# A list scheduler that also orders the opening pair of token blocks, with table loads and a transfer limit in its model

## The chip, the cores and the metric

The kernel runs on one core of one Trainium2 chip. The metric is device time in microseconds (us): the median of the runs of one kernel. Each run takes one launch; nothing is computed on the host but layouts.

## What is computed

B = 4 batches, N = 6080 tokens, C = 256 channels. The reference, cut to what matters:

```python
qn = q / (norm(q, axis=1) + 1e-6)          # over the 6080 tokens
kn = k / (norm(k, axis=1) + 1e-6)
s  = kn.transpose(0, 2, 1) @ qn / tau      # 256 x 256 for each batch
a  = exp(s - s.max(-1));  a /= a.sum(-1) + 1e-9
x  = (v @ a).reshape(24320, 256)
h  = x @ w_in                              # w_in 256 x 2048, float64
g  = 0.5 * h * (1 + erf(h / sqrt(2)))
out = g @ w_out                            # w_out 2048 x 256, float64
```

## The kernel before, in words

**Numbers in two parts.** Each float32 operand is split into a high and a low part of a narrower type (fp32r), and a product is three matmuls: lo x hi, hi x hi and hi x lo. The two weight matrices arrive as float64, and are narrowed on the device into such pairs by *narrow steps* on DVE and ACT (L522 to L539: clamp, square, integer masks and shifts, cast, subtract, add; the results are `wi`, `win` or `wo`). A narrow step's temporary is `nt` at first and later, by turns, `kqc` and `osb`.

**Folding the attention away.** Batch b's softmax matrix (256 x 256) is multiplied into w_in (`w_group(b, g)`: products L717 to L719 into PSUM, scaling L722, split into `wh`/`wl` at L709/L710, further sums and splits L748 to L761). So a token block needs only v times this product, gelu, and the product with w_out.

**The order of the work.** First come the raw loads, norms and scores of batch 0 (loads L395, products L421, copies of `po` L440) and its softmax, up to about 63 us. Then:

1. `w_group(0, 0)`, then *pair 0*: the first two blocks of 512 tokens of batch 0, computed by plain products. It is done in 8 units u, one for each 256 of the 2048 hidden columns: `plain_products(u)` (L836 to L838, operands `vhi` and `wh`/`wl`), gelu into a high part (L845) and in full (L846) on ACT, the low part `los` on DVE (L847), and one unit later `pair_out(u)` (L970 to L972, with the output weights `wo`). Between the units stand narrow steps for the weights still wanted (`narrow_unit`, `load_unit` for the raw loads at L505) and `w_group(0, 1..3)`. The finished weights are also written to HBM: `keep_in` and `keep_out` (L1096).
2. The *plan*: all other token blocks, chunk by chunk and column group by column group, with a fast seven-product form of matrix multiplication (`chunk_ops` L892 to L894; sums on DVE; gelus L919 and L922; `chunk_out` L1009 to L1011 and L1025 to L1027). The first chunk of the plan is (0, 2). While it runs, DVE makes forms of the output weights (L587) that are kept in `keep_out` and later read by `load_part` (L571) through a ring of four `wo` buffers, 503 loads of 512 KB. `win` is loaded by `load_win` (L551), v by `load_v` (L781). Scores and softmax of batches 1 to 3 are spread over it; softmax needs ACT's Exp (L669) and Sqrt, the blocks need Gelu, and these live in different activation tables.

**What sets the order.** Up to the plan, the order on each engine comes from the order of emission, from `tc.high_priority()` and from `behind(mark)`, which lets a group be issued only after a marked instruction. The plan's instructions are then reordered by class `Order`: `learn` assigns names to ring slots, `arrange` collects dependences (ring slots among them) and costs from `cost`, with PE kept in program order; `latest` derives deadlines backwards from PE's nominal times; `run` does list scheduling over PE, ACT, DVE and SP, in which a transfer takes its bytes by BANDWIDTH and DMA_LAT ns of latency, and transfers run one behind the other; `schedule` repeats it 24 times with deadlines moved ahead where PE stalled, and takes the best. The result is fixed as dependences of each instruction on the one ahead of it on its engine. Instructions of the plan come behind everything emitted earlier on their engine.

Of the kernel before, what the change touches and what calls it, by code (L numbers as in the profile page):

```python
# [78 lines left out]
class Order:  # L79
# [32 lines left out]
    def cost(self, ins, reads, writes):  # L112
        n = max([x[3] for x in reads + writes] + [1])
        psum = any(x[0][0] in ("pa", "pb", "px", "pz", "po0", "po1", "po2", "po3") for x in reads)
        if ins.engine == PE:
            k = reads[0][3] if reads else 1
            if ins.ins[0].dtype == F32:
                return (max(1.69 * k, 112.0),) * 2
            return .4167 * k + 3 + 1.5 * (k <= H), .4167 * k + 170
        if ins.engine == DVE:  # L120
            t = n / .96 + 66
            if type(ins).__name__ == "InstTensorCopy" and not psum:
                t = n / 1.92 + 66
            return t, t + 90
# [58 lines left out]
    def schedule(self, todo, preds, costs):  # L183
# [4 lines left out]
        self.preds, self.costs = preds, costs  # L188
        self.succs = [[] for _ in range(n)]
# [56 lines left out]
    def run(self, late):  # L246
# [5 lines left out]
        for a in range(n):  # L252
            if not left[a]:
                known[self.engine[a]].append(a)
        free, order, slip, dma, events = [0.0] * 4, [], 0.0, 0.0, [0.0]
        while len(order) < n:
# [3 lines left out]
            for e in range(4):  # L260
                if free[e] > now or not known[e]:
                    continue
# [15 lines left out]
                free[e] = now + self.costs[pick][0]  # L278
# [5 lines left out]
                for b, d in self.edges[pick]:  # L284
                    t = dma + DMA_LAT / 2 if d is None else now + d
# [13 lines left out]
BANDWIDTH, DMA_LAT, DMA_LATE = 320.0, 2000, 6000  # L299
# [26 lines left out]
def channel_attention_gelu_ffn(ctx, tc, qk, kqt, vt, tau, w_in, w_out, out):  # L326
# [222 lines left out]
    def load_win(b, g):  # L549
        new_win(b, g)  # L550
        nc.sync.dma_start(out=f32(wins[b, g]), in_=keep_in[g])  # L551
# [226 lines left out]
    def load_v(b, p):  # L778
        t0, n = PAIRS[p]
        raw = pv.tile([P, NCT, 2 * NT], F32, name="v_raw")  # L780
        nc.sync.dma_start(out=raw[:, :, :2 * n],  # L781
                          in_=vt[:, b * N + t0:b * N + t0 + 2 * n].rearrange("(t p) n -> p t n", p=P))
        vraw[b, p] = raw
# [391 lines left out]
    with tc.high_priority(), behind("fill"):  # L1175
        w_group(0, 0)
# [5 lines left out]
    def extras(w):  # L1182

        if w in (0, 2, 4):
            with behind("product"):
                w_group(0, w // 2 + 1)
# [14 lines left out]
    for u in range(NU):  # L1201
# [4 lines left out]
        for _ in range(paces[u] if u < len(paces) else 0):  # L1206
            with behind(*(["gelu"] if u == 0 else [])):
                narrow_unit()
# [224 lines left out]
    body = nc.cur_bb.bb.instructions  # L1433
    start = len(body)
# [4 lines left out]
    todo, preds, costs = order.arrange(list(body), start)  # L1439
    latest = {e: [i.name for i in list(body)[:start] if i.engine == e] for e in (PE, ACT, DVE, SP)}  # L1440
# [43 lines left out]
```

## Time and profile before

| | |
|---|---|
| median of 3 runs (lowest, highest) | 2091.68 us (2085.11, 2091.8) |
| the profiled execution, its own time | 2087.38 us |
| its span | 2085.4 us (2.0 lie around it) |
| mean granted TensorE clock | 0.995 |
| instructions | 40663 |
| PE, DVE, ACT busy | 2039.9, 1857.6, 1621.0 us |
| moved by DMA | 475.30 MB, mean 228 GB/s |

PE is TensorE's matmul, PEld its weight load, DVE VectorE, ACT ScalarE, SP the engine that issues all transfers (`SPq` its queue). A row of the timeline gives start, duration, engine, line, operation, output <- input with shape, and in brackets the idle time ahead of it with what ended it. In a table of waits, "PE po L970 <- DVE wo L539: 4.4, 1, 4.4" says that PE's products for `po` at L970 waited for DVE's `wo` made at L539 for 4.4 us in total, once, at most 4.4. PEclk is the granted TensorE clock, 1.00 being full speed. Line numbers in rows of before are those of the kernel before; in the changed kernel the same lines stand 8 to 12 further down.

### The profile page before, as it was taken

To read this page: it belongs to the slowest core of one execution; us is meant where nothing else is said; L and a number is where in the kernel's file an instruction comes from. 1 tells how busy PE (TensorE), PEld (TensorE's weight loads), DVE (VectorE), ACT (ScalarE), POOL (GpSimd) and SP (SyncE) were. 2 spreads that over 40 slices of the span, in tenths; PEclk is the share of its full clock that TensorE was granted. 3 is DMA by queue.
4 is the path that set the end of the run, shared out by engine and by line. 5 is a ranking of instruction groups with operands and counts; after the bars stand their busy time and mean duration, and the time that the engine had idled before them with its cause. 6 is when DMAs were issued, how large, how long until landed. Compare 5 with 4: busy or idle time off the path is not lost.

```text
span 2085.4 us, 40663 instructions
## 1 busy us (share of the span) xinstructions
PE 2039.9 (98%) x15958; PEld 1967.0 (94%) x15958; DVE 1857.6 (89%) x2733; ACT 1621.0 (78%) x2718; POOL 1.3 (0%) x8
## 2 busy tenths in 40 slices
PE   9889999999999999999999999999999999999999
PEld 7778899999999999999999999999999999999999
DVE  6997899998899999999889899999988998898897
ACT  6665788888888888887888777777787777777775
POOL 0000000000000000000000000000000000000000
PEclk9999999999999999999999999999999999999999
DMA  9547777777777678777687666666556556566655
GB/s 377 183 126 249 238 272 242 270 260 251 251 270 267 223 250 272 238 265 245 211 278 263 206 217 215 219 209 212 199 175 219 183 195 209 196 197 211 198 191 165
DMA packets 151695, 475.30 MB, mean 228 GB/s; under 512 B 15440, under 2 KB 25680, under 8 KB 149456
## 3 DMA queue, kind: packets, MB, share of 16 engines
q1 hardware_dynamic: 151504, 472.71, 67.0%
q8 instruction: 125, 2.05, 0.4%
q14 instruction: 66, 0.54, 0.1%
HBM read 435.16 MB, written 37.49 MB: 227 GB/s over the span
## 4 chain that ended last, share of the span: by engine, by line
PE 83%; DVE 7%; ACT 4%; DMA 4%; issue 2%; SPq 0%; DVEq 0%; ACTq 0%
PE po L1027 9%; PE po L1026 9%; PE po L1025 9%; PE pb L892 4%; PE pb L894 4%; PE pb L893 4%; PE pa L892 4%; PE pa L894 4%; PE pa L893 4%; PE po L1009 3%; PE po L1011 3%; PE po L1010 3%; PE pz L894 2%; PE pz L893 2%; PE pz L892 2%; DMA v_raw<-vt 2%
## 5 line engine op out<-in xcount | busy, mean ns | idle before, releaser
L1027 PE MATMUL po<-los,wo 128*128 128x256 f32 (+1 forms) x1890 | 520.9, 276 | 1.0 <-DVE los L943 0.8
L1025 PE MATMUL po<-his,wo 128*128 128x256 f32 (+1 forms) x1890 | 520.5, 275 | 0.8 <-issue 0.8
L1026 PE MATMUL po<-his,wo 128*128 128x256 f32 (+1 forms) x1890 | 520.0, 275 | 0.0
L925 DVE TENSOR_TENSOR los<-gs,his 128x512 fp32r<-128x512 f32 (+1 forms) x601 | 406.7, 683 | 83.0 <-ACT gs L919 71.0
L1025 PEld LDWEIGHTS po<-his,wo 128*128 128x128 f32 x1890 | 362.9, 192 | 2.8 <-ACT e L669 0.9
L1027 PEld LDWEIGHTS po<-los,wo 128*128 128x128 f32 x1890 | 363.1, 192 | 2.0 <-DVE los L943 1.5
L1026 PEld LDWEIGHTS po<-his,wo 128*128 128x128 f32 x1890 | 363.1, 192 | 0.5
L943 DVE TENSOR_TENSOR los<-gs,his 128x1024 fp32r<-128x1024 f32 (+1 forms) x270 | 326.7, 1211 | 16.3 <-ACT his L939 14.0
L939 ACT CAST his<-gs 128x1024 fp32r<-128x1024 f32 (+1 forms) x270 | 281.3, 1043 | 64.6 <-DVE gs L936 59.5
L892 PE MATMUL pa<-vhi,wl 128*128 128x256 f32 (+1 forms) x920 | 254.2, 276 | 8.1 <-ACT gs L919 7.3
L892 PE MATMUL pb<-vhi,wl 128*128 128x256 f32 (+1 forms) x920 | 254.6, 277 | 4.8 <-DVE pz L906 1.4
L893 PE MATMUL pb<-vhi,wh 128*128 128x256 f32 (+1 forms) x920 | 253.4, 275 | 0.0
L894 PE MATMUL pa<-vlo,wh 128*128 128x256 f32 (+1 forms) x920 | 253.3, 275 | 0.0
L893 PE MATMUL pa<-vhi,wh 128*128 128x256 f32 (+1 forms) x920 | 253.3, 275 | 0.0
L894 PE MATMUL pb<-vlo,wh 128*128 128x256 f32 (+1 forms) x920 | 253.3, 275 | 0.0
L932 DVE TENSOR_TENSOR gs<-gs 128x1024 f32<-128x1024 f32 (+1 forms) x135 | 163.8, 1214 | 31.6 <-ACT gs L919 27.5
L892 PEld LDWEIGHTS pa<-vhi,wl 128*128 128x128 f32 x920 | 176.5, 192 | 13.4 <-ACT gs L919 8.3
L922 ACT ACTIVATE his<-px 128x512 fp32r<-128x512 f32 (+1 forms) x184 | 109.0, 592 | 101.7 <-PE px L894 98.6
L892 PEld LDWEIGHTS pb<-vhi,wl 128*128 128x128 f32 x920 | 176.7, 192 | 10.0 <-DVE pz L906 2.6
L893 PEld LDWEIGHTS pa<-vhi,wh 128*128 128x128 f32 x920 | 176.6, 192 | 3.7
L893 PEld LDWEIGHTS pb<-vhi,wh 128*128 128x128 f32 x920 | 176.7, 192 | 2.5
L894 PEld LDWEIGHTS pb<-vlo,wh 128*128 128x128 f32 x920 | 177.0, 192 | 0.0
(284 smaller groups left out, 5147.3 us busy)
## 6 DMA issues: line engine op xcount, KB each, us to landing
wo<-keep_out SPq DMA_DIRECT2D x503, 512.0 KB, 4.4
raw<-qk SPq DMA_DIRECT2D x95, 512.0 KB, 6.4
kqc<-kqt SPq DMA_DIRECT2D x72, 512.0 KB, 5.1
wo<-keep_out SPq DMA_DIRECT2D x135, 256.0 KB, 3.9
v_raw<-vt SPq DMA_DIRECT2D x20, 1024.0 KB, 7.7
out<-osb SPq DMA_DIRECT2D x40, 512.0 KB, 5.1
win<-keep_in SPq DMA_DIRECT2D x12, 1024.0 KB, 7.4
keep_in<-win SPq DMA_DIRECT2D x4, 1024.0 KB, 4.5
```

What stands on the lines that cost most here:

```text
L892: nc.tensor.matmul(o, wls[g][:, a, q], paired(vh[:, at, :h]), start=start, stop=False, skip_group_check=True)
L893: nc.tensor.matmul(o, whs[g][:, a, q], paired(vh[:, at, :h]), start=False, stop=False, skip_group_check=True)
L894: nc.tensor.matmul(o, whs[g][:, a, q], paired(vl[:, at, :h]), start=False, stop=stop, skip_group_check=True)
L922: nc.scalar.activation(out=slot(name)[0], in_=t[SOURCE[name]], func=AF.Gelu)
L925: tt(out=slot(name)[1], in0=whole(name), in1=f32(slot(name)[0]), op=ALU.subtract)
L932: tt(out=g4[:, 0:2], in0=g4[:, 1:3], in1=g4[:, 0:2], op=ALU.subtract)
L939: nc.scalar.copy(out=views[1][:, 2 - 2 * i:4 - 2 * i], in_=views[0][:, 2 * i:2 * i + 2])
L943: tt(out=views[2][:, at], in0=views[0][:, 2 * i:2 * i + 2], in1=f32(views[1][:, at]), op=ALU.subtract)
L1009: nc.tensor.matmul(o, w[:, 1, q], mh, start=start, stop=False, skip_group_check=True)
L1025: nc.tensor.matmul(o, w[:, 1, q], mh, start=starts and q == 0, stop=False, skip_group_check=True)
L1026: nc.tensor.matmul(o, w[:, 0, q], mh, start=False, stop=False, skip_group_check=True)
L1027: nc.tensor.matmul(o, w[:, 0, q], ml, start=False, stop=stops and q == 1, skip_group_check=True)
```

## The change

Five things, in 142 lines of diff:

1. The scheduled part begins at `w_group(0, 0)` (`opened`) instead of at the plan. `high_priority` and `behind` are dropped from `w_group(0, *)` and `narrow_unit`; PE follows the order of emission there, and ACT, DVE and SP follow the scheduler. What was emitted before `opened` stays ahead on each engine.
2. `cost`: PE's matmul never takes less than 111.7 ns; every DVE operation that reads at most one wide operand, and none in PSUM, counts at the double rate, where only copies did.
3. ACT's switches between Gelu, Exp and Sqrt cost TABLE = 1290 ns in the scheduler's time. No rule groups them; the instruction behind a switch, and what depends on it, are just reckoned later by that much.
4. A transfer's latency counts as 3000 ns instead of 2000 (7000 instead of 6000 in the deadlines), and SP issues nothing while the transfers under way, as modelled, need more than BACKLOG = 2200 ns.
5. `load_win` and `load_v` are two transfers each.

```diff
-            return .4167 * k + 3 + 1.5 * (k <= H), .4167 * k + 170
+            return max(.4167 * k + 2.8, 111.7), .4167 * k + 170
...
-            if type(ins).__name__ == "InstTensorCopy" and not psum:
+            if len([x for x in reads if x[3] > 1]) < 2 and not psum:
                 t = n / 1.92 + 66
...
+        self.table = [str(getattr(i, "func", "")).rsplit(".", 1)[-1] if type(i).__name__ == "InstActivation" else "" for i in todo]
+        self.table = [x if x in ("Gelu", "Exp", "Sqrt") else "" for x in self.table]
...
+        table = "Gelu"
...
+                if e == 3 and dma > now + BACKLOG:
+                    heapq.heappush(events, dma - BACKLOG)
+                    continue
...
-                free[e] = now + self.costs[pick][0]
+                began = now
+                if self.table[pick] not in ("", table):
+                    table = self.table[pick]
+                    began = now + TABLE
+                free[e] = began + self.costs[pick][0]
...
-                    t = dma + DMA_LAT / 2 if d is None else now + d
+                    t = dma + DMA_LAT / 2 if d is None else began + d
...
-BANDWIDTH, DMA_LAT, DMA_LATE = 320.0, 2000, 6000
+BANDWIDTH, DMA_LAT, DMA_LATE, TABLE, BACKLOG = 320.0, 3000, 7000, 1290, 2200
...
-        nc.sync.dma_start(out=f32(wins[b, g]), in_=keep_in[g])
+        for i in range(2):
+            nc.sync.dma_start(out=f32(wins[b, g][:, i]), in_=keep_in[g][:, i])
...
-    with tc.high_priority(), behind("fill"):
-        w_group(0, 0)
+    body = nc.cur_bb.bb.instructions
+    opened = len(body)
+    w_group(0, 0)
...
-            with behind("product"):
-                w_group(0, w // 2 + 1)
+            w_group(0, w // 2 + 1)
...
-            with behind(*(["gelu"] if u == 0 else [])):
-                narrow_unit()
+            narrow_unit()
...
-    todo, preds, costs = order.arrange(list(body), start)
+    todo, preds, costs = order.arrange(list(body), opened)
```

PE's order is all but the same (some 30 of 15836 rows move), DVE has the same 2735 instructions, ACT has 21 table loads in place of 19, SP 995 transfers in place of 959.

**SP, at the start of the new scheduled part.** `raw_w` and `raw` are raw loads of the float64 weights, `keep_in` and `keep_out` the writes of finished ones, `v_raw` the load of v. Before:

```order
L505 DMA raw_w<-w_out 128x1024
L1096 DMA keep_in_98<-win 128x2048
L505 DMA raw<-w_out 128x1024
L505 DMA raw<-w_in 128x1024 x2
L1096 DMA keep_in_99<-win 128x2048
L1096 DMA keep_out_102<-wo 128x2x128 x4
L781 DMA v_raw<-vt 128x2x1024
L505 DMA raw<-w_out 128x1024 x2
```

The same place now:

```order
L515 DMA raw_w<-w_out 128x1024
L1107 DMA keep_in_98<-win 128x2048
L1107 DMA keep_in_99<-win 128x2048
L1107 DMA keep_out_102<-wo 128x2x128 x4
L515 DMA raw<-w_out 128x1024
L515 DMA raw<-w_in 128x1024 x2
L793 DMA v_raw<-vt 128x1024 x2
L515 DMA raw<-w_out 128x1024
```

Three raw loads, the first `raw<-w_out` and two `raw<-w_in`, have moved behind a `keep_in` and four `keep_out` writes, which read the narrowed weights `win` and `wo`.

**DVE, ahead of the output weights of unit 4.** `kqc` and `osb` are the temporaries of two narrow steps, `los` is a low part of gelu's result, `wl` a low part of the folded weights. Before:

```order
L529 SCALAR_TENSOR_TENSOR raw<-raw,osb 128x512
L529 SCALAR_TENSOR_TENSOR raw<-raw,kqc 128x512
L531 SCALAR_TENSOR_TENSOR osb<-osb,raw 128x512
L531 SCALAR_TENSOR_TENSOR kqc<-kqc,raw 128x512
L847 TENSOR_TENSOR los<-gs,his 128x512
L534 TENSOR_SCALAR raw<-osb 128x512
L534 TENSOR_SCALAR raw<-kqc 128x512
L535 SCALAR_TENSOR_TENSOR osb<-raw 128x512
L538 TENSOR_TENSOR osb<-osb,wo 128x512
L535 SCALAR_TENSOR_TENSOR kqc<-raw 128x512
L539 TENSOR_TENSOR wo<-osb 128x512
```

Now:

```order
L539 SCALAR_TENSOR_TENSOR raw<-raw,osb 128x512
L549 TENSOR_TENSOR win<-kqc 128x512
L541 SCALAR_TENSOR_TENSOR osb<-osb,raw 128x512
L858 TENSOR_TENSOR los<-gs,his 128x512
L544 TENSOR_SCALAR raw<-osb 128x512
L545 SCALAR_TENSOR_TENSOR osb<-raw 128x512
L548 TENSOR_TENSOR osb<-osb,wo 128x512
L549 TENSOR_TENSOR wo<-osb 128x512
L858 TENSOR_TENSOR los<-gs,his 128x512
L772 TENSOR_TENSOR wl_497<-hl,wh_496 128x1024
```

The two narrow steps, that took turns instruction by instruction, now come one behind the other, and a wide `wl` split stands behind the `wo` (before, three of them stand ahead of it in the queue, now one).

**ACT, in the softmax of batch 2.** `e` is Exp's result, `his` and `gs` are gelu's. Before:

```order
L669 ACT_TABLE_LOAD
L669 ACTIVATE e_11741,small<-t_11401,small 128x256
L824 CAST vhi<-v_raw 128x2x240
L492 ACTIVATE kqc,nsum<-kqc 128x1024
L922 ACT_TABLE_LOAD
L922 ACTIVATE his<-px 128x2x240
L919 ACTIVATE gs<-px 128x2x240
L669 ACT_TABLE_LOAD
L669 ACTIVATE e_11743,small<-t_11403,small 128x256
L922 ACT_TABLE_LOAD
L922 ACTIVATE his<-p_11727 128x2x240
```

Now:

```order
L680 ACT_TABLE_LOAD
L680 ACTIVATE e_11758,small<-t_11417,small 128x256
L933 ACT_TABLE_LOAD
L933 ACTIVATE his<-px 128x2x240
L930 ACTIVATE gs<-px 128x2x240
L933 ACTIVATE his<-p_11744 128x2x240
L930 ACTIVATE gs<-p_11744 128x2x240
L933 ACTIVATE his<-pz 128x2x240
L930 ACTIVATE gs<-pa 128x2x240
L930 ACTIVATE gs<-pz 128x2x240
L680 ACT_TABLE_LOAD
L680 ACTIVATE e_11760,small<-t_11419,small 128x256
```

The number of table loads around the two Exps stays; between them now stand seven gelu instructions instead of two, and behind the second Exp copies and casts, which need no table, come ahead of the next load for Gelu.

More of the change, by code (lines that the diff above doesn't have):

```diff
@@ L780, in load_v @@
         raw = pv.tile([P, NCT, 2 * NT], F32, name="v_raw")
-        nc.sync.dma_start(out=raw[:, :, :2 * n],
-                          in_=vt[:, b * N + t0:b * N + t0 + 2 * n].rearrange("(t p) n -> p t n", p=P))
+        for k in range(NCT):
+            nc.sync.dma_start(out=raw[:, k, :2 * n], in_=vt[k * P:(k + 1) * P, b * N + t0:b * N + t0 + 2 * n])
         vraw[b, p] = raw
@@ L1431, in channel_attention_gelu_ffn @@
     assert not [x for x in later.values() if x], {k: len(x) for k, x in later.items() if x}
-    body = nc.cur_bb.bb.instructions
-    start = len(body)
     order = Order()
@@ L1438, in channel_attention_gelu_ffn @@
     order.learn(list(body))
-    todo, preds, costs = order.arrange(list(body), start)
-    latest = {e: [i.name for i in list(body)[:start] if i.engine == e] for e in (PE, ACT, DVE, SP)}
+    todo, preds, costs = order.arrange(list(body), opened)
+    latest = {e: [i.name for i in list(body)[:opened] if i.engine == e] for e in (PE, ACT, DVE, SP)}
     for at in order.schedule(todo, preds, costs):
```

## The prediction

> **What bounds the kernel now.** I read the page's first part, then busy time by stretches, then PE's waits in the two stretches that the second view marks, and last single rows around the waits. The page gives the span and each engine's share of it:
>
> ```profile
> span 2085.4 us, 40663 instructions
> PE 2039.9 (98%) x15958; PEld 1967.0 (94%) x15958; DVE 1857.6 (89%) x2733; ACT 1621.0 (78%) x2718; POOL 1.3 (0%) x8
> ```
>
> PE is busy for 98% of the span and its products stay the same, so at most the other 45 us, and time at a lowered clock, can be won. The stretches (length; busy us of PE, PEld, DVE, ACT, POOL; PEclk, DMA share, GB/s) say where that time lies:
>
> ```profile
> 60.00:90.00 30.00, 24.53 (x104) 20.32 (x104) 27.50 (x54) 20.42 (x38) 0.00 (x0) 0.94 0.45 146
> 90.00:130.00 40.00, 37.79 (x172) 31.80 (x170) 40.00 (x68) 25.79 (x44) 0.00 (x0) 1.00 0.44 147
> 130.00:165.00 35.00, 31.11 (x134) 26.90 (x135) 28.77 (x51) 19.97 (x36) 0.00 (x0) 0.90 0.36 106
> 165.00:240.00 75.00, 66.76 (x443) 60.93 (x442) 58.29 (x103) 48.24 (x86) 0.00 (x0) 0.98 0.75 259
> 240.00:2085.00 1845.00, 1824.98 (x14867) 1780.74 (x14865) 1659.87 (x2391) 1469.39 (x2467) 0.00 (x0) 1.00 0.68 227
> ```
>
> From 60 to 240, the stretch that the scheduler newly takes in or starts with, PE is idle for 5.5 + 2.2 + 3.9 + 8.2 = 19.8 us, and a clock below 1 costs 0.06 x 30 + 0.10 x 35 + 0.02 x 75 = 6.8 us more: 26.6 in all. From 240 on, 20.0 us are idle in 1845. DVE is busy for all 40 us from 90 to 130, so there it is DVE that PE follows. PE's longest waits from 60 to 240 (total, times, longest):
>
> ```profile
> PE po L970 <- DVE wo L539: 4.4, 1, 4.4
> PE po L1011 <- DVE los L925: 3.8, 1, 3.8
> PE po L970 <- ACT his L845: 3.4, 1, 3.4
> PE pa L836 <- DVE wl L710: 1.2, 1, 1.2
> PE po L1009 <- DMA wo<-keep_out: 1.1, 1, 1.1
> ```
>
> Each occurs once: it is not a rhythm but single places in which DVE (narrowed weights, splits) or a transfer was late.
>
> **The change part by part.** (a) The new scheduled part starts at w_group(0,0), with units and narrow steps behind it. These are DVE's rows there now, and PE's pace in a plain product:
>
> ```profile
> 63.48 1.13 DVE L710 TENSOR_TENSOR wl<-hl,wh 128x256 fp32r<-128x256 f32 x3
> 65.86 0.45 DVE L440 COPY sacc<-po 128x256 f32<-128x256 f32 x1
> 69.05 0.44 DVE L522 TENSOR_SCALAR raw<-raw 128x512 f32<-128x512 f32 x1
> 79.77 0.38 PE L836 MATMUL pz<-vhi,los 128*128 128x512 f32 x1
> 79.99 0.38 PE L837 MATMUL pz<-vhi,his 128*128 128x512 f32 x1
> ```
>
> Everything emitted ahead of the scheduled part stays ahead of it on its engine. By the changed order the three wl (1.0), two copies of po (0.7) and one L522 (0.3, its next start) are no longer ahead of the wo<-nt whose successor starts at 69.05, so it is done at 69.05 - 2.0 = 67.0; but the first wl now comes behind it, at 67.4. PE's first products for pair 0 start at 67.5 instead of 63.9, where the first of the three wl ends now. Now PE starts early and stalls (the 1.2 and the 3.4 above); then it would stand in one piece of some 4.7. Four blocks of six products at 0.216 (79.99 - 79.77) are 5.2 us. They end now at 63.9 + 5.2 + 1.2 + 3.4 = 73.7 and 1 to 1.8 for the lowered clock, and then at 67.5 + 5.2 + an estimated 1.5 for the clock = 74.2: a gain of about 0.5 (bounds -1.5 to 3), which counts only if PE doesn't wait for DVE further on.
>
> (b) SP moves three weight loads behind keep_in_99 and the four keep_out writes, which wait for DVE's narrowed weights:
>
> ```profile
> 69.21 1.97 SPq L1096 DMA_DIRECT2D keep_out<-wo  x4
> DMA to landing us min/median/max: 3.4/6.6/11.3
> ```
>
> The first row is the issue of the four writes, the second the narrow loads' time from issue to landing (L505). With wo at 67.0 SP is through the writes at 67.1 + 2.0 = 69.1; the load lands at 69.1 + 3.4 = 72.5 at best, by the median at 75.7. Its data lies there from about 62 now. DVE's ninth instruction of the new part is the L532 that needs it; it gets there at about 68.7 and waits 3.8 (bounds 0, if the order runs later than I add it up, to 7), with the los of unit 0 queued behind it.
>
> (c) DVE's path to the output weights of unit 4, for which PE waits 4.4. The rows: a window from the last L522 above to the end of that wo, the six integer steps of a narrow unit, a los, a wl, and the wo:
>
> ```profile
> 69.05:133.84 64.79, 56.69 (x249) 47.85 (x249) 62.29 (x111) 45.35 (x78) 0.00 (x0) 0.96 0.44 140
> 79.08 0.87 DVE L529 SCALAR_TENSOR_TENSOR raw<-raw,osb 128x512 uint32<-128x512 uint32 x1
> 79.85 0.83 DVE L531 SCALAR_TENSOR_TENSOR kqc<-kqc,raw 128x512 f32<-128x512 f32 x1
> 81.36 0.48 DVE L534 TENSOR_SCALAR raw<-kqc 128x512 uint32<-128x512 uint32 x1
> 81.72 0.51 DVE L534 TENSOR_SCALAR raw<-osb 128x512 uint32<-128x512 uint32 x1
> 88.60 1.34 DVE L847 TENSOR_TENSOR los<-gs,his 128x512 fp32r<-128x512 f32 x2
> 89.85 1.23 DVE L761 TENSOR_TENSOR wl<-hl,wh 128x1024 fp32r<-128x1024 f32 x1
> 133.12 0.72 DVE L539 TENSOR_TENSOR wo<-osb 128x512 fp32r<-128x512 f32 x1
> ```
>
> Of 64.8 us DVE is busy for 62.3. In the new order two narrow units are no longer interleaved: six steps of the other one, three at 0.77 (79.85 - 79.08) and three at 0.36 (81.72 - 81.36), come behind this wo: -3.4. Two of three wide wl move behind it (2 x 1.14 from start to start: -2.3), and three los (3 x 0.62: -1.9). What (a) deferred comes in: +2.0. That is 56.7. With 3.8 for (b) and an estimated 1.5 of the 2.5 us of other idle time, the wo is there at 67.0 + 56.7 + 3.8 + 1.5 = 129.0, against 133.8: 4.8 earlier. PE could need it at 74.2 + 7.8 (36 products of w_group(0,1)) + 41.5 (four units of 48 at 0.216) + 0.6 = 124.1, so PE still waits for DVE here, and the gain is DVE's 4.8. If (b) costs nothing and all idle time goes, the wo comes at 123.7 and PE sets the pace; if the load takes 11.3, nothing is won. The next wo comes at 139.1 by the same sums, and PE wants it 48 products later, at 129.0 + 10.4 = 139.4, so that wait is covered by little. The 0.5 of (a) lies ahead of that wait and is not added. Of the lowered clock (1.8 us lost from 60 to 90, 3.5 from 130 to 165) I take 1.2 as won, since the wait behind which it falls grows no longer than 4.9: the gain from 60 to 165 is 6, bounds 0 to 10.7.
>
> (d) From 165 to 240 PE loses 8.2 + 1.5 = 9.7. Two rows, the burst of transfers and the weight forms' wait:
>
> ```profile
> 170.00:180.00 10.00, 9.27 (x63) 8.34 (x62) 7.37 (x10) 7.67 (x13) 0.00 (x0) 1.00 1.01 412
> 217.76 1.10 DVE L587 TENSOR_TENSOR osb<-wo 128x256 f32<-128x256 f32 x3 [2.55 <-DMA keep_out<-osb]
> ```
>
> The transfers stand at a share of 1.01 here; the new limit on transfers under way moves two win loads of 1 MB (2.5 us each at 412 GB/s) out of this burst, so the wo that is 1.1 late now should be in time. The forms' buffer comes free when its write has landed; in the new order 5.1 to 5.5 us of other DVE work stand between such steps, 1.8 to 4.1 before, so idle pieces like this 2.55 shrink, and with them the 3.8 for los L925. I take half, 5 (bounds 0 to 9).
>
> (e) The scheduler now counts ACT's table switches. PE's waits from 240 on that lie beside such switches (softmax of batches 1 to 3, totals), the group, two rows of ACT, the wait, and two stretches:
>
> ```profile
> PE pa L892 <- ACT gs L919: 7.3, 5, 3.2
> PE po L1011 <- DVE los L925: 1.1, 1, 1.1
> PE pb L892 <- ACT his L922: 1.1, 1, 1.1
> L922 ACT ACT_TABLE_LOAD x6 | 7.7, 1283 | 0.1
> 1029.66 1.28 ACT L922 ACT_TABLE_LOAD   x1
> 1030.95 0.60 ACT L922 ACTIVATE his<-p 128x480 fp32r<-128x480 f32 x1
> 1030.00:1040.00 10.00, 6.98 (x49) 6.99 (x50) 7.55 (x13) 9.12 (x16) 0.00 (x0) 0.83 0.32 88
> 1150.00:1160.00 10.00, 8.40 (x47) 7.26 (x47) 6.32 (x16) 8.87 (x14) 0.00 (x0) 0.83 0.56 194
> ```
>
> The waits come to 9.5 and the two lowered clocks to 2 x 0.17 x 10 = 3.4: 13 us. At 1030 three loads stand within seven instructions of ACT's queue, unplanned 3 x 1.28 = 3.8 us of delay, and PE stands for 3.2. The new order keeps seven gelus together between such loads and lets copies and casts, which need no table, follow Exp; it has 21 loads in place of 19. Two more cost ACT 2.6 us, and PE none as long as ACT's 22% idle time lies beside them. I take 8 of the 13 (bounds 3 to 13).
>
> The Trainium skill (ScalarE: Activation LUTs, What ACT_TABLE_LOAD costs) adds to the 1283 ns a drain of some 1380, 2.66 us a switch, and under Rules for kernel authors tells one to batch activations by table set. It speaks against an order with two loads more; by it the two would take 5.3 us of ACT. Here the gelu starts at 1030.95, 0.01 behind the load's end, so this trace shows no drain behind the load.
>
> The first of the two stretches has the lowered clock behind an idle piece of 3.2; the second shows as much (0.83) although PE is busy for 8.40 of its 10 us and the longest wait in it is the 1.1 of the los row, so small waits close together cost the clock too. The Trainium skill (TensorE: Matmul & The Clock Gate, Part 1: The HAM clock gate (the "warmup" mystery)) has PE at half rate behind an idle window of some 3.4 us; by it the second stretch would have kept its clock, and 1.7 less could be won in (e). The second stretch disagrees.
>
> (f) New costs for PE and DVE change only choices between ready instructions. The 36 more transfers (halves of win and v) cost SP 0.3 to 0.5 us each to issue. In the steady part I take 0 for both, bounds -4 to 4, some 40% of the 20.0 - 9.5 = 10.5 us of idle time there that (e) does not hold.
>
> The sum: 6 + 5 + 8 = 19. The profiled execution took 2087.4 (span 2085.4, 2.0 around it), so 2068.4 for a profile. The median of the runs is 4.3 above it, the fastest run 2.3 below; runs spread more than that one profile shows, and I add 1.6: **2070**.
>
> **The rivals.** *The stalls only move.* DVE has no slack from 60 to 165, and by (b) the weight loads come 3.4 to 11.3 later than SP is free. The scheduler's clock starts with all engines free at w_group(0,0), while DVE is in truth busy up to 67 us: an order tuned for the wrong start need not do what the change says. Then (c) and (d) give 0 to 2 and (e) half, 3 to 6: 2081 to 2087 by the same addition. For it: 40.00 of 40 busy. Against it: the 3.4 + 2.3 + 1.9 = 7.6 us of DVE steps that move are counted from its own queue.
>
> *All gaps close.* (c) 10.7, (d) 9, (e) 13, and 3 of the other 10.5 us: 36 off, 2052. For it: each wait is a single place. Against it: DVE's fixed busy time from 69 to 134.
>
> *SP becomes the bound, and the kernel slower.* The steady part streams its output weights through four buffers, and SP issues in order:
>
> ```profile
> SPq L571 <- PE po L1027: 973.2, 520, 7.1
> SPq L400 <- DVE hl L457: 119.2, 59, 6.6
> wo<-keep_out SPq DMA_DIRECT2D x503, 512.0 KB, 4.4
> ```
>
> A wo load waits for PE to free its buffer (520 times) and lands 4.4 us from issue. A step uses four in about 10.3 us, 2.6 each, so a freed buffer is wanted again 3 x 2.6 = 7.8 us later: 3.4 us to spare. Where a transfer ahead in SP's queue waits longer than 3.4 for another engine, PE waits the difference; L400 waits up to 6.6 already. The changed order, with a limit that holds transfers back, would make this regular: a wait of 4.4 in its place is 1 us over; at each of some 46 chunks that is +46, and with the 19 still won 2087.4 - 19 + 46 = 2114. For it: 36 more issues, and writes pulled ahead of loads in (b). Against it: PE shows no wait for wo in 1845 us now, and longer transfers are what the scheduler newly reckons with.
>
> **How the numbers follow.** 0.3% of the time is 6.3 us, and that is about what a measurement of this kernel can tell from no change. Main forecast 0.60: its own range by the bounds of (c), (d), (e) is 2058 to 2081. Stalls only move 0.22: half of it within 0.3% of 2091.7, half below 2085. All gaps close 0.09. Slower by SP 0.09. Faster: 0.60 + 0.11 + 0.09, less 0.03 for medians that lie as far apart as the runs shown (2085.1 to 2091.8), 0.77; within 0.3%: 0.14; slower 0.09. The range leaves out the slower rival and most of the closing of all gaps: 2056 to 2086.
>
> **What would show it.** Right: in the changed profile PE waits once for wo near 129 and stands 4 to 5 us ahead of its first plain product; DVE waits some 4 us for a weight load near 69; from 170 on no wait for wo<-keep_out; PE's waits for gs beyond 240 sum to under 4 us and PEclk stays at 1.00 near both softmax stretches. (b) is wrong if that load comes in time, (c) if the wait for wo is still near 134, (e) if the sum of the waits for gs stays at 7. The prediction as a whole fails if PE's idle time from 240 on grows over 24 us (SP's rival), or falls from 60 to 240 by under 5.

## The result, and the profile after

| | before | changed |
|---|---|---|
| median (runs) | 2088.43 us (4: 2085.11 to 2091.8) | 2062.45 us (4: 2061.83 to 2062.77) |
| profiled execution, its span | 2087.38, 2085.4 | 2062.65, 2060.9 |
| table loads in ACT's order | 19 | 21 |

The ratio is 0.9875, 95% interval 0.9853 to 0.9897: 26 us faster, where 20 or so were forecast (2070). The interval lies beyond 0.3%. One execution of one kernel below, that with switches at 0 and 67 ns, ran at a mean granted clock of 0.556 and took 3505.99 us; it is left out of that kernel's median. The page of the changed kernel, its busy times by the same stretches as before, and PE's longest waits, first from 60 to 240, then from 240 on:

```profile
span 2060.9 us, 40753 instructions
PE 2032.2 (99%) x15958; PEld 1962.3 (95%) x15958; DVE 1857.9 (90%) x2733; ACT 1620.7 (79%) x2720; POOL 1.3 (0%) x8
```

```profile
60.00:90.00 30.00, 25.52 (x103) 20.52 (x103) 25.57 (x50) 21.34 (x38) 0.00 (x0) 0.89 0.46 157
90.00:130.00 40.00, 36.92 (x168) 31.18 (x167) 39.71 (x67) 24.16 (x42) 0.00 (x0) 1.00 0.54 169
130.00:165.00 35.00, 35.00 (x157) 29.97 (x157) 34.41 (x58) 23.73 (x42) 0.00 (x0) 0.95 0.67 214
165.00:240.00 75.00, 69.83 (x479) 64.80 (x478) 66.27 (x114) 51.41 (x88) 0.00 (x0) 0.98 0.66 219
240.00:2060.00 1820.00, 1811.99 (x14822) 1771.71 (x14821) 1650.42 (x2382) 1464.92 (x2464) 0.00 (x0) 1.00 0.69 230
```

```profile
PE pa L847 <- DVE wl L721: 4.2, 1, 4.2
PE pa L903 <- DVE pz L917: 3.4, 2, 3.0
PE pa L729 <- DVE win L549: 2.2, 1, 2.2
PE po L1022 <- DVE los L936: 1.7, 1, 1.7
PE po L981 <- DVE wo L549: 0.9, 2, 0.6
```

```profile
PE pb L903 <- ACT gs L930: 1.3, 1, 1.3
PE pb L903 <- ACT his L933: 1.1, 1, 1.1
PE pa L903 <- DVE pz L917: 1.0, 3, 0.5
```

PE's idle time from 60 to 240 is now 4.5 + 3.1 + 0 + 5.2 = 12.7 us in place of 19.8; from 240 on it is 8.0 in place of 20.0. The larger part of the gain thus lies in the steady part, far from pair 0. (The wait of 3.4 for `pz` is new; it comes back under (d).)

To see where the time goes, both executions are cut at the same work: where PE has started 244, 528 and 1000 instructions and begins the next, and where its last, of 15958, begins. The first cut lies ahead of the new scheduled part; the second is past the output weights of unit 4; the third is past the first chunk of the plan. The last piece is parted once more: five stretches of PE's work, its instructions 3100 to 3500, 5400 to 6500, 7300 to 7600, 7900 to 9400 and 11400 to 11600, are so wide that the table loads of every kernel below fall into them beyond cut 1000. They are added up as "at the switches" (before, they lie at 487 to 540, 777 to 913, 1010 to 1052, 1089 to 1279 and 1525 to 1553 us); what is left of the piece is "the rest". Other bounds for the five move a gain at the switches by 1 to 2 us. The expectations below speak of 16 us there; they go by narrower stretches, with bounds that aren't on record.

| us | before | changed | gain |
|---|---|---|---|
| start to 244 | 59.6 | 62.2 | -2.6 |
| 244 to 528 | 78.3 | 74.4 | 3.9 |
| 528 to 1000 | 90.9 | 87.1 | 3.7 |
| 1000 to the end | 1852.6 | 1833.1 | 19.5 |
| of it: at the switches | 448.8 | 435.4 | 13.4 |
| of it: the rest | 1403.8 | 1397.7 | 6.1 |

The first four add up to 24.5, the difference of the two spans. The first 2.6 are only partly the change's: the three kernels below whose instructions up to there are those of before (67 ns, 65 ns, switches alone) took 61.2, 60.2 and 61.1 us for that piece, so the execution of before that was profiled was a quick one there. The seven kernels that open at `w_group(0, 0)` took 61.4 to 62.7, so about 1 us may belong to the opening; through what isn't settled.

The steps of (a) and (b) can be seen one by one: PE's wait for the first `wl`, DVE's for the raw load, and the weights for unit 4:

```profile
69.58 0.80 PE L847 MATMUL pa<-vhi,wl 128*128 128x512 f32 x1 [4.17 <-DVE wl L721]
```

```profile
69.25 1.96 SPq L1107 DMA_DIRECT2D keep_out<-wo  x4
71.25 0.49 SPq L515 DMA_DIRECT2D raw<-w_out  x1
```

```profile
68.50 0.69 DVE L549 TENSOR_TENSOR wo<-nt 128x512 fp32r<-128x512 f32 x1
...
75.40 0.57 DVE L532 TENSOR_SCALAR raw<-raw 128x512 f32<-128x512 f32 x1 [3.57 <-DMA raw<-w_out]
...
132.20 0.69 DVE L549 TENSOR_TENSOR wo<-osb 128x512 fp32r<-128x512 f32 x1
```

PE stands in one piece of 4.2; SP issues the load behind the four writes, which wait for `wo`; DVE waits 3.6 for it. All three were forecast (4.7, that order, 3.8). But the weights of unit 4 are ready at 132.9, not at 129.0.

Around 1012, where before has the wait of 3.2, ACT's rows and the two stretches of 10 us that hold the work for which before showed a clock of 0.83:

```profile
1012.56 1.28 ACT L680 ACT_TABLE_LOAD   x1
1013.86 0.51 ACT L680 ACTIVATE e<-t,small 128x256 f32<-128x256 f32 x1
...
1014.48 1.28 ACT L933 ACT_TABLE_LOAD   x1
...
1019.18 1.28 ACT L680 ACT_TABLE_LOAD   x1
```

```profile
1010.00:1020.00 10.00, 10.00 (x73) 9.47 (x72) 8.90 (x18) 9.89 (x17) 0.00 (x0) 1.00 0.38 133
1135.00:1145.00 10.00, 10.00 (x75) 9.52 (x74) 9.53 (x21) 9.96 (x19) 0.00 (x0) 1.00 0.66 213
```

There are as many loads as before in this place, but PE is busy for all of 10 us and the clock stays at 1.00. So far all of it agrees with the prediction's (e). Whether the counting of the switches did it is what the runs below ask.

### The profile page after: what moved, and what is told of

Read it like the earlier page. It is cut to its first block, busy times and chain, and to the rows that moved or that the text cites. A ratio compares the mean times of both kernels' runs of the same rounds, so it can differ in the third digit from the quotient of the medians.

```text
span 2060.9 us, 40753 instructions
## 1 busy us (share of the span) xinstructions
PE 2032.2 (99%) x15958; PEld 1962.3 (95%) x15958; DVE 1857.9 (90%) x2733; ACT 1620.7 (79%) x2720; POOL 1.3 (0%) x8
## 4 chain that ended last, share of the span: by engine, by line
PE 87%; DVE 6%; DMA 3%; ACT 2%; issue 1%; SPq 0%; DVEq 0%; ACTq 0%
PE po L1038 10%; PE po L1037 10%; PE po L1036 10%; PE pb L903 5%; PE pb L904 5%; PE pb L905 5%; PE pa L903 5%; PE pa L904 5%; PE pa L905 5%; PE po L1020 4%; PE po L1022 4%; PE po L1021 4%; DMA raw<-qk 2%; PE pz L904 2%; PE pz L905 2%; PE pz L903 2%
## 5 line engine op out<-in xcount | busy, mean ns | idle before, releaser
L905 PEld LDWEIGHTS pa<-vlo,wh 128*128 128x128 f32 x920 | 176.8, 192 | 0.0
```

Source lines behind the costliest of these rows:

```text
L905: nc.tensor.matmul(o, whs[g][:, a, q], paired(vl[:, at, :h]), start=False, stop=stop, skip_group_check=True)
```

## The experiments

The theory after the comparison: the counted switches save PE's waits at the softmaxes, and the opening is worth the 4 to 8 us from 60 to 229. The rivals: the new costs, latencies and the transfer limit save it; fewer table loads would be better; the opening wins nothing. The first four kernels add or take away one part each; before was run beside them again (median 2089.02, 11 runs).

**Switches at 0 in the changed kernel.**

```diff
-BANDWIDTH, DMA_LAT, DMA_LATE, TABLE, BACKLOG = 320.0, 3000, 7000, 1290, 2200
+BANDWIDTH, DMA_LAT, DMA_LATE, TABLE, BACKLOG = 320.0, 3000, 7000, 0, 2200
```

> The changed kernel with the cost of a table switch set to 0 in the scheduler, nothing else changed; its order has 15 table loads where the changed kernel has 21 and the kernel before 19. Theory (the scheduler's knowledge of the switches is what saves PE beside the softmaxes of batches 1 to 3, whatever the number of loads): 2072 to 2079, with 8 to 16 us of waits for ACT and of lowered clock back between 480 and 1660. Rival A (the new costs, latencies and the transfer limit save it): 2062 to 2065. Rival B (fewer loads are better): 2050 to 2061, since six loads less are 7.7 us of ACT.

Measured: 2065.99 (2064.22 to 2066.43), ratio to before 0.9891 (0.9872 to 0.9909). The theory's 2072 to 2079 is missed, and rival A's 2062 to 2065 by 1 us. Of the 13.4 us at the switches this kernel, which knows nothing of them, keeps 9.3 (439.6 us against before's 448.8). Beyond 240 its PE waits more for gelu (5.0 where the changed kernel has 1.6), which is what is left of the theory:

```profile
PE pa L903 <- ACT gs L930: 5.0, 4, 1.5
```

Rival B falls too: 15 loads are no faster than 21.

**Counted switches alone, on the kernel before.**

```diff
+        table = "Gelu"
...
+                began = now
+                if self.table[pick] not in ("", table):
+                    table = self.table[pick]
+                    began = now + TABLE
-                free[e] = now + self.costs[pick][0]
+                free[e] = began + self.costs[pick][0]
...
-BANDWIDTH, DMA_LAT, DMA_LATE = 320.0, 2000, 6000
+BANDWIDTH, DMA_LAT, DMA_LATE, TABLE = 320.0, 2000, 6000, 1290
```

> The kernel before with the counting of table switches alone (1290 ns), the scheduled part begins at the plan, costs, latencies, transfers as before. Theory: it wins most of the 16 us that lie beside the softmaxes, 2070 to 2078, PE's waits for gs beyond 240 under 3 us. Rival A: 2085 to 2091, waits for gs near 7.

Measured: 2074.42 (2072.65 to 2076.36), ratio 0.9931 (0.9915 to 0.9947). As the theory had it, and its wait for gs is 1.3 beyond 240. By itself this would have passed for a proof. But the run above, without the count, lost most of the same stalls, so the count isn't needed for that.

**The opening alone, on the kernel before.**

```diff
-    with tc.high_priority(), behind("fill"):
-        w_group(0, 0)
+    body = nc.cur_bb.bb.instructions
+    opened = len(body)
+    w_group(0, 0)
...
-    todo, preds, costs = order.arrange(list(body), start)
+    todo, preds, costs = order.arrange(list(body), opened)
```

(`behind` goes at the other two places as well.)

> The kernel before with the scheduled part opened at w_group(0,0), nothing else. Theory: the opening is worth what lies between 60 and 165, some 4 us by the comparison of the two traces, perhaps with part of the 4 between 165 and 240: 2080 to 2086; DVE waits 3 to 4 us for a raw load near 72 and PE stands 4 us ahead of its first plain product, as in the changed kernel; waits for gs beyond 240 stay near 7. Rival C (the opening is what makes the steady part better, because the state in which it begins differs): under 2075.

Measured: 2078.55 (2076.53 to 2082.97), ratio 0.9953 (0.9937 to 0.997). That is 1.5 below the theory's 2080 to 2086 and not under rival C's 2075. PE's waits from 60 to 240, and DVE's for the load:

```profile
PE pa L836 <- DVE wl L710: 4.2, 1, 4.2
PE po L970 <- DVE wo L539: 3.0, 2, 2.6
PE pa L718 <- DVE win L539: 2.5, 1, 2.5
PE pa L836 <- DVE wl L761: 2.2, 1, 2.2
PE pb L836 <- ACT gs L846: 1.8, 1, 1.8
```

```profile
DVE raw L522 <- DMA raw<-w_out: 3.4, 1, 3.4
```

The stall at the start and the late load are there (4.2 and 3.4), but from cut 244 to 528 it takes 81.5, 3.2 longer than before: with the old model the opening makes pair 0 worse. It wins 8.3 from 528 to 1000, and 6.3 in the steady part, about which the edit brings no knowledge; all of the 6.3 lies at the switches (442.3 against 448.8). The stretch with the wait of 3.2 near 1030 (instructions 7300 to 7600) takes 37.5 us here against 41.6. That made me suspect the order itself.

**The changed kernel with the plan alone scheduled.**

```diff
-    body = nc.cur_bb.bb.instructions
-    opened = len(body)
-    w_group(0, 0)
+    with tc.high_priority(), behind("fill"):
+        w_group(0, 0)
...
+    body = nc.cur_bb.bb.instructions
+    opened = len(body)
     order = Order()
```

(`behind` is put back at the other two places as well.)

> The changed kernel with the scheduled part beginning at the plan again, and pair 0 in the order of before. Theory: it keeps the gain beside the softmaxes and loses that of the opening, 2064 to 2068; the 4.4 us wait for the output weights of unit 4 is back near 134. Rival D (the opening wins nothing because its stall at the start and its late load take back what it orders better): 2060 to 2063.

Measured: 2063.24 (2061.83 to 2064.88), ratio 0.9878 (0.9862 to 0.9895). That lies between the theory's 2064 to 2068 and rival D's 2060 to 2063, nearer to D: the opening is worth 0.8, less than can be told. The pieces show why: 244 to 528 takes 79.3 (changed kernel 74.4), with the old waits back (that of 4.4 until 135.9),

```profile
PE po L981 <- DVE wo L549: 4.4, 1, 4.4
PE po L981 <- ACT his L856: 3.4, 1, 3.4
```

and 528 to 1000 takes 84.9 in place of 87.1, the later part 1834.3 in place of 1833.1. So the opening wins 4.9 in pair 0 and 1.2 in the later part, and hands 2.2 back in the first chunk and 1.5 ahead of cut 244. By the spans that leaves 2.2 in these two profiles (the one of the kernel without it is its slowest run, 2064.88), by the medians 0.8.

**One nanosecond.** An edit without knowledge, on the kernel before:

```diff
-            t = n / .96 + 66
+            t = n / .96 + 67
```

> The kernel before with DVE's fixed cost in the scheduler's model at 67 ns instead of 66, an edit that carries no knowledge; its order has 15 table loads where before has 19. Theory 'luck' (the old model doesn't see the switches, so that which of the five softmax stretches stall is an accident of ties, which any edit redraws): 2075 to 2095, at least one of the stretches near 1030, 1155 and 1540 changes by over 2 us, up or down. Rival 'rule' (the stalls belong to the old rules, and only the counted switch or the new costs remove them): 2086 to 2091, each stretch within 1 us of before.

Measured: 2074.28 (2072.48 to 2076.04), ratio 0.9931 (0.9917 to 0.9945). That is 0.7 below the theory's range and far from the rival's. The edit that carries nothing wins 14 us, as much as the counted switches alone; the stretch near 1030 takes 38.4 us in place of 41.6. Its wait for gs beyond 240, ACT's rows and the two stretches:

```profile
PE pa L892 <- ACT gs L919: 1.9, 3, 1.0
```

```profile
1020.37 1.28 ACT L669 ACT_TABLE_LOAD   x1
1021.67 0.51 ACT L669 ACTIVATE e<-t,small 128x256 f32<-128x256 f32 x1
...
1022.62 0.51 ACT L669 ACTIVATE e<-t,small 128x256 f32<-128x256 f32 x1
...
1025.26 1.28 ACT L922 ACT_TABLE_LOAD   x1
```

```profile
1025.00:1035.00 10.00, 9.11 (x72) 8.53 (x71) 8.63 (x17) 9.38 (x18) 0.00 (x0) 1.00 0.83 291
1145.00:1155.00 10.00, 9.84 (x74) 9.09 (x74) 8.85 (x18) 9.54 (x15) 0.00 (x0) 1.00 0.74 245
```

Both Exps happen to stand between the same two loads. The clock is whole in both stretches, and at the switches it takes 436.4 us (before 448.8, changed kernel 435.4).

**And one nanosecond less.**

```diff
-            t = n / .96 + 66
+            t = n / .96 + 65
```

> The kernel before with DVE's fixed cost in the model at 65 ns, the other side of the 67 that took 2074.3; 15 table loads again. Theory 'luck' (before's order is an unlucky draw among ties): 2070 to 2082, the time from 229 to the end 1838 to 1846 us where before has 1852.6 and the 67 ns version 1839.7. Rival (67 ns was the lucky one, before is what the old model gives as a rule): 2085 to 2091, and 1850 to 1854.

Measured: 2070.97 (2067.64 to 2073.09), ratio 0.9922 (0.9905 to 0.9938); the part from cut 1000 on takes 1837.3, at the switches 436.9. The total is in the theory's range, the later part just below its 1838 to 1846 and far from the rival's 1850. Of three orders that the old model gives for 65, 66 and 67 ns, the kernel before has the worst by 14 to 17 us.

**The changed kernel, one nanosecond off, and the same with switches at 0.**

```diff
-            t = n / .96 + 66
+            t = n / .96 + 67
```

> The changed kernel with DVE's fixed cost at 67 ns instead of 66; its ACT order differs from the changed kernel's in 192 rows, where the same edit moved 449 in before. Theory (the new model knows what decides, so ties decide less): 2060 to 2066, and 1831 to 1836 us from 229 of before's work to the end (changed kernel 1833.1). Rival (luck rules here as well, and the changed kernel was a good draw): 2068 or more, or 1838 or more for that part.

Measured: 2061.36 (2060.83 to 2061.88), ratio 0.9872 (0.9858 to 0.9887), the later part 1833.6, at the switches 436.7; total and later part are as the theory had them. The new model's two orders lie 1.1 us apart, the old model's three 17.

> The changed kernel with table switches at 0 and DVE's fixed cost at 67 ns: a second draw of the version that took 2066.0. Theory (counting the switches is worth 3 to 4 us once costs and transfers are right): 2064 to 2069, 1836 to 1840 us in the later part. Rival (those 3.5 us were luck): 2060 to 2063.

Measured (the same edit, with TABLE at 0): 2066.93 (2065.59 to 2067.36, three runs), ratio 0.9898 (0.9881 to 0.9914). The execution left out is the profiled one, so the later part stays unmeasured. With 2065.99 this makes two versions without the switches against 2062.45 and 2061.36 with them: counting them is worth 3.5 and 5.6 us, 4.6 on the mean, inside the new model.

**Old transfer model, old costs.** Each in the changed kernel:

```diff
-BANDWIDTH, DMA_LAT, DMA_LATE, TABLE, BACKLOG = 320.0, 3000, 7000, 1290, 2200
+BANDWIDTH, DMA_LAT, DMA_LATE, TABLE, BACKLOG = 320.0, 2000, 6000, 1290, 1e12
```

> The changed kernel with latencies of 2000 and 6000 ns again and no limit of transfers under way; switches counted, new costs, opening and halved loads kept. Theory (the transfer model pays only where transfers are dense, 137 to 229): it loses 1 to 4 us there and nothing beside the softmaxes, 2063 to 2067. Rival A (longer latencies are what keeps the steady part free of waits): 2070 or more, with waits beyond 240 for transfers or for work that hangs on them.

Measured: 2065.15 (2064.95 to 2067.33), ratio 0.9891 (0.9875 to 0.9906): 2.7 lost. The size is the theory's, the place isn't: from 528 to 1000 it takes 83.3, 3.8 less than the changed kernel; it loses 1.6 from 244 to 528 and 5.3 in the later part (1838.4), 2.3 of them at the switches and 3.0 in the rest.

```diff
-            return max(.4167 * k + 2.8, 111.7), .4167 * k + 170
+            return .4167 * k + 3 + 1.5 * (k <= H), .4167 * k + 170
...
-            if len([x for x in reads if x[3] > 1]) < 2 and not psum:
+            if type(ins).__name__ == "InstTensorCopy" and not psum:
```

> The changed kernel with the old costs of PE and DVE in the model; switches counted, new latencies, limit, opening and halved loads kept. Theory (costs choose between ready instructions only): 2061 to 2066, the softmax stretches as in the changed kernel. Rival A' (DVE's truer costs save what the switches don't, since the kernel with switches at 0 lost only 3.5): 2068 to 2076, with the loss from 60 to 165, where DVE is the bound, and in the steady part.

Measured: 2071.0 (2069.11 to 2074.22), ratio 0.9917 (0.9903 to 0.9932): 8.6 lost, the rival's. From 244 to 528 it takes 80.0 (changed kernel 74.4), where PE waits for win and wo as in the kernel with the opening alone,

```profile
PE pa L729 <- DVE win L549: 3.8, 2, 2.7
PE po L981 <- DVE wo L549: 3.1, 1, 3.1
```

and the later part takes 1841.3 (1833.1): 1.3 of the 8.2 lie at the switches, 6.9 in the rest. Of the parts taken away one by one, the truer costs are the largest. That is one order, and under the old costs one nanosecond moved the time by 14 us or more; but what it moved lies mostly at the switches. The rest took 1400.4 to 1403.8 us in those three orders, as the table of pieces below shows, 1404.6 here and 1397.7 in the changed kernel.

**The raw loads first.** Writes of finished weights wait for the scheduled part, so SP issues the loads ahead of them:

```diff
-        if (1, FILL - 1) not in raws and not marks.get("kept"):
+        if "open" not in state:
...
-    for x in held:
-        keep(*x)
...
     for _ in range(3):
         load_unit()
+    state["open"] = True
+    for x in held:
+        keep(*x)
```

> The changed kernel with the writes of finished weights held back until the scheduled part, so that SP issues the three raw loads ahead of them; w_group(0,0) stays in the scheduled part. Theory (the late load is a cost of its own, of about 3 us): DVE's wait of 3.6 near 72 goes, PE's 4.4 near 69 stays, win and wo near 130 come some 3 earlier, 2058 to 2061. Rival (w_group(0,0) behind DVE's narrow steps is what costs, and the load is hidden behind it): 2062 to 2064.

Measured: 2060.89 (2059.01 to 2063.15), ratio 0.9871 (0.9856 to 0.9885): in the theory's band, but 1.6 from the changed kernel is less than can be told. Its trace says that the late load was half hidden; PE's waits from 60 to 165, DVE's from 60 to 100, and the weights of unit 4:

```profile
PE pa L847 <- DVE wl L721: 4.1, 1, 4.1
PE pa L729 <- DVE win L549: 2.3, 1, 2.3
```

```profile
DVE los L858 <- ACT gs L857: 2.7, 3, 1.4
```

```profile
130.72 0.69 DVE L549 TENSOR_TENSOR wo<-osb 128x512 fp32r<-128x512 f32 x1
```

DVE's wait for the load is gone, but now DVE waits 2.7 for gelu, because PE's first product is still 4.1 late: the next cause in line stands right behind the one removed. The weights of unit 4 come 1.5 earlier than in the changed kernel, and PE waits for win as long as there.

**Opening the scheduled part one step later.** `w_group(0, 0)`, at high priority again, and the three loads behind it are emitted ahead of it:

```diff
-    body = nc.cur_bb.bb.instructions
-    opened = len(body)
-    w_group(0, 0)
+    with tc.high_priority(), behind("fill"):
+        w_group(0, 0)
     for _ in fill:
         pass
     for _ in range(3):
         load_unit()
+    body = nc.cur_bb.bb.instructions
+    opened = len(body)
```

> The changed kernel with w_group(0,0) and the three raw loads behind it emitted ahead of the scheduled part, at high priority as before. Theory (SP's new order costs DVE 3.6 us of waiting near 72, and PE's one piece of 4.4 near 69 is paid in before's two pieces of 1.5 and 3.6): DVE no longer waits for a raw load, the weights win and wo that PE waits for near 130 come 3 us earlier, 2058 to 2061. Rival (what DVE wins is lost again ahead of the plan, or the stretch from 137 to 229 is bound by something else): 2062 to 2064.

Measured: 2055.65 (2054.95 to 2056.62), ratio 0.9843 (0.9828 to 0.9858). It beats the changed kernel by 6.8 us, more than expected. PE's waits from 60 to 165, the weights of unit 4, and the busy times:

```profile
PE px L847 <- issue: 4.4, 1, 4.4
PE pa L847 <- DVE wl L721: 1.2, 1, 1.2
PE pa L729 <- DVE win L549: 0.8, 1, 0.8
```

```profile
127.49 0.69 DVE L549 TENSOR_TENSOR wo<-osb 128x512 fp32r<-128x512 f32 x1
```

```profile
60.00:90.00 30.00, 24.44 (x106) 20.54 (x105) 28.49 (x55) 21.39 (x39) 0.00 (x0) 0.94 0.41 135
130.00:165.00 35.00, 34.78 (x172) 29.97 (x171) 34.54 (x56) 25.42 (x44) 0.00 (x0) 1.00 0.59 181
165.00:240.00 75.00, 71.22 (x517) 66.87 (x517) 66.14 (x114) 54.18 (x93) 0.00 (x0) 1.00 0.73 240
```

PE's start is in two pieces again (1.2, and 4.4 for which the profile shows no releaser), DVE waits for no raw load, the weights of unit 4 are there at 128.2, 4.7 earlier than in the changed kernel, and the wait for win falls from 2.2 to 0.8. The piece from 244 to 528 takes 71.5 (changed kernel 74.4), that from 528 to 1000 84.6 (87.1), the later part is the same (1833.2); 2.1 us lie ahead of cut 244 (60.1, where the orders that begin the scheduled part at the plan took 59.6 to 61.2). The larger share of this isn't a shorter wait: PE's idle time from 60 to 240 is 11.4 us against 12.7, but the clock, which is at 0.89, 0.95 and 0.98 in these three stretches of the changed kernel, is at 0.94, 1.00 and 1.00 here. That is 1.8 us of PE's time lost to it in place of 6.6.

The pieces side by side (us; each from that kernel's one profiled execution; medians of the runs at the right):

| kernel | to 244 | 244-528 | 528-1000 | 1000-end | at the switches | the rest | loads | median |
|---|---|---|---|---|---|---|---|---|
| before | 59.6 | 78.3 | 90.9 | 1852.6 | 448.8 | 1403.8 | 19 | 2088.4 |
| before, 67 ns | 61.2 | 79.5 | 89.4 | 1839.7 | 436.4 | 1403.3 | 15 | 2074.3 |
| before, 65 ns | 60.2 | 76.5 | 87.8 | 1837.3 | 436.9 | 1400.4 | 15 | 2071.0 |
| before + switches | 61.1 | 78.3 | 87.2 | 1840.8 | 437.0 | 1403.8 | 21 | 2074.4 |
| before + opening | 61.5 | 81.5 | 82.6 | 1846.3 | 442.3 | 1404.0 | 17 | 2078.6 |
| changed | 62.2 | 74.4 | 87.1 | 1833.1 | 435.4 | 1397.7 | 21 | 2062.5 |
| changed, 67 ns | 61.4 | 74.5 | 86.5 | 1833.6 | 436.7 | 1396.9 | 21 | 2061.4 |
| switches at 0 | 61.4 | 74.2 | 85.7 | 1837.2 | 439.6 | 1397.6 | 15 | 2066.0 |
| old transfers | 61.9 | 76.0 | 83.3 | 1838.4 | 437.7 | 1400.7 | 19 | 2065.2 |
| old costs | 62.7 | 80.0 | 82.2 | 1841.3 | 436.7 | 1404.6 | 21 | 2071.0 |
| plan alone | 60.7 | 79.3 | 84.9 | 1834.3 | 435.4 | 1398.9 | 21 | 2063.2 |
| raw loads first | 61.7 | 73.6 | 84.9 | 1834.6 | 436.9 | 1397.7 | 21 | 2060.9 |
| opened later | 60.1 | 71.5 | 84.6 | 1833.2 | 435.5 | 1397.7 | 21 | 2055.7 |

Every order but before's own and the opening's alone comes to 435 to 440 at the switches, with the switches counted or not. The rest goes largely by the model: the six orders that keep the old costs take 1400.4 to 1404.6 there, the one with new costs and old transfers 1400.7, and the six with both new 1396.9 to 1398.9.

## Why the prediction was right, and where it wasn't

The direction, the range and the bound (PE's idle places, not its work) were right; the median came out 7.6 below the forecast. That it came so near is in good part luck: the terms of the sum were right in other proportions than they were set down, and the largest came true for another reason than the one given, by (e) below.

**(a) and (b)** held as steps: 4.2 of standing against 4.7, 3.6 of waiting for the load against 3.8, at the places named. What (a) left out is that its late start is handed on: PE's first gelu inputs come later, and DVE waits for ACT. It was seen only when the load was moved (2.7).

**(c)** was mis-sized. It had 6, with the wo of unit 4 at 129.0; measured are 132.9 for that wo and, from cut 244 to 528, 3.9. Its 1.2 for the clock didn't come: from 60 to 165 that costs 5.1 us now (0.11 x 30 + 0.05 x 35) and 5.3 before. Of the 3.9 us by which the wo is late, 2.9 lie ahead of DVE's end of waiting (75.4 in place of 72.5): the wo that SP's writes wait for is done at 69.2 and not at 67.0, in an execution that was 2.6 behind before's already at cut 244, and the load is there 4.2 after its issue where 3.4 were taken. The other 1.0 lie in the chain behind it (57.5 us from 75.4 to 132.9, where 56.7 + 1.5 - 1.7 = 56.5 were added up). So the adding of DVE's queue from rows was good to 1 us in 57; what it started from wasn't. Where I had named a wait of PE for wo as a sign, there was one for win, 2.2 us long, near 129, and none for the wo of unit 4: another result of the same queue, which I hadn't followed. The 139.1 for the wo behind it and the bound of 10.7 stand in the prediction without their working.

**(d)** had 5, and 3.7 came from cut 528 to 1000. The transfers' share from 170 to 180 is down and the wo is no longer late; the forms' idle piece is half as long, but PE still waits behind the forms, now for `pz`:

```profile
170.00:180.00 10.00, 9.57 (x65) 8.64 (x64) 8.30 (x16) 6.69 (x13) 0.00 (x0) 1.00 0.86 292
```

```profile
213.62 1.10 DVE L598 TENSOR_TENSOR osb<-wo 128x256 f32<-128x256 f32 x3 [1.32 <-DMA keep_out<-osb]
```

```profile
218.10 0.38 PE L903 MATMUL pa<-vhi,wl 128*128 128x256 f32 x1 [3.00 <-DVE pz L917]
```

That limiting the transfers does it, as (d) said, is contradicted: with the old transfer model the share from 170 to 180 is 0.74, and the piece is 3.8 shorter still (83.3). The kernels with some part of the change come to 82.2 to 87.2 there (before's own orders to 87.8 to 90.9). What makes the changed one slower than that with old transfers can be read: from 165 to 240 its PE is idle for 5.2 us, 1.7 for `los` and 3.0 for `pz`, at a clock of 0.98, and there for 1.6 us, at 1.00. So of the 3.8 for `los` that (d) meant to halve, 3.0 are left under another name. Why the order puts the forms ahead of that `pz` stays open.

**(e)** is the step that failed in its reason. It said that the scheduler, since it counts the switches, would win 8 of 13 us there. The five stretches at the switches won 13.4; but 12.4 and 11.9 are won there by an edit of one nanosecond up or down, with no switch counted. The kernel before was one unlucky order among several that its model can't tell apart, and each of the four edits of it that were tried leaves it. Under the old model the count adds nothing to that: 437.0 at the switches with it, 436.4 and 436.9 without. What counting the switches adds was seen only inside the new model: 4.6 us of median over two pairs of kernels; in the pair with profiles, 4.2 us at the switches. That the stalls would go because two loads more are placed better also fell: orders with 15 loads take 436.4 to 439.6 at the switches, those with 21 take 435.4 to 437.0. The profile of before showed these stalls as single places of different length with no rhythm; that could have told me that they might be accidents of an order, not the price of a rule.

**(f)** had 0 for the new costs, "change only choices between ready instructions". Taken away alone they cost 8.6 us; between the two profiles it is 5.6 from 244 to 528, where DVE sets the pace, 8.2 in the later part and 0.5 ahead, less 4.9 from 528 to 1000. Of the 8.2, 6.9 lie in the rest, for which the prediction took 0 and which won 6.1. It was wrong to price at nothing the numbers by which the scheduler chooses on an engine that was busy for 40.00 of 40 us.

The rivals: *the stalls only move* was right for one part, the opening (2063.2 without it); its remark that the scheduler takes all engines as free at `w_group(0, 0)` fits what opening later won (6.8 us), though the runs don't separate the wrong starting state from the priority that `w_group(0, 0)` got back. *SP becomes the bound* didn't occur: beyond 240 no wait for `wo` stands among PE's longest. *All gaps close* named 2052, and 12.7 and 8.0 us of idle time are left.

What each part is worth, then: from the old model's other two orders (2071.0 and 2074.3) to the changed kernel it is 9 to 12 us; costs come to 8.6, switches to 4.6, transfers to 2.7 and the opening to 0.8 where each is taken away alone; they don't add up, since each also redraws the order. The remaining 14 to 17 of the 26 us are the leaving of before's order. The halved loads by themselves, and the latencies apart from the transfer limit, weren't tried.

## What to carry to other kernels

Before crediting a rule of a scheduler with a gain, change a number of it that means nothing, by the least amount, in the kernel before and in the one after: here 1 ns moved the old order by 14 to 17 us, and the new one, in the one direction tried, by 1. Price the cost model itself where the engine it orders has no slack, and follow a queue that is moved behind another wait to the next one that depends on it. Try more than one place to open a scheduled part: one step later was worth 6.8 us here, though it isn't shown whether by the state that the scheduler assumes or by the priority of what stands ahead. Keep loads that nothing holds back ahead of writes that wait: here that took away a wait of 3.6, of which the next wait in line took the larger part back.

## What the runs showed of the hardware

The kernel before varies between 2083.7 and 2093.4 in 11 runs beside the first four experiments (0.5%), the changed one between 2061.8 and 2062.8 in 4; what makes an order vary so wasn't looked into. The first piece, with the same instructions in the same order in before and its two one-nanosecond versions, took 59.6, 61.2 and 60.2 us. The granted clock can fall without a long wait: in before, PE is busy for 1.80 of the 3.4 us from 1152.2 to 1155.6, its longest wait in them is 1.1, and in the 3.4 us behind the clock is 0.51; with 9.11 busy of 10 us from 1025 to 1035 the 67 ns version keeps 1.00. And no wait shows behind a table load: the activation behind the load at 1012.56 starts at 1013.86, the end of its 1.28 us and 0.02 more.
